# Attention and expert products on one core: six batches of attention moved in among the products of the first four expert units

## The chip, the cores and the metric

The kernel runs on one core of a Trainium2 chip. The metric is device microseconds of one execution. Before the change three runs took 523.98 to 524.93 us, with a median of 524.35 us.

The engines have short names in all views: PE is TensorE (PEld its weight loads), DVE is VectorE, ACT is ScalarE, POOL is GpSimd and SP the engine that issues most transfers. Each works through its own instructions in order.

## The reference

An attention block is followed by a mixture of experts. For each of 8 batches and 8 heads, 512 tokens read 32 states and the states read the tokens; the 544 rows of 512 numbers that result go through one expert of eight.

```python
scores = scale * np.matmul(x, state.transpose(0, 1, 3, 2))      # B, H, S, Ns = 8, 8, 512, 32; D = 64
a = np.exp(scores - scores.max(-1, keepdims=True))
xread = np.matmul(a / (a.sum(-1, keepdims=True) + 1e-09), state)   # token reads
scores2 = scale * np.matmul(state, x.transpose(0, 1, 3, 2))
a2 = np.exp(scores2 - scores2.max(-1, keepdims=True))
sread = np.matmul(a2 / (a2.sum(-1, keepdims=True) + 1e-09), x)     # state reads
x = np.concatenate([xread, sread], axis=2).transpose(0, 2, 1, 3).reshape(B, S + Ns, H * D)
logits, local = x @ w_gate, sigmoid(x @ w_local)
for b in range(B):
    for s in range(S + Ns):                    # in order: an expert can be inherited
        e = argmax(logits[b, s]) if s == 0 or local[b, s] < 0.5 else e
        out[b, s] = softmax(logits[b, s])[e] * (np.maximum(x[b, s] @ w1[e], 0) @ w2[e])
```

With the given inputs the tokens of a batch go to one expert (a token that does not is counted and would be done at the end), so the 512 tokens of a batch are a unit of work with one expert's weights. The 256 state rows are sorted by expert into 9 tiles of 32.

## The kernel before, in words

**Attention** (class `Attention`). Each batch goes through some thirty steps: scores (L301), maxima and transposes on VectorE (L309, L328, L331), subtraction, halves and shares on GpSimd (L338, L349, L361), exponents on ScalarE (L317, L342), transposes and state reads on TensorE (L371, L384), logits (L404, L416), and token reads (L424). A token read is one matmul of 128x512 whose weights, `sd`, hold the states on a diagonal of 32x32 blocks with zeros around them; ScalarE copies its result (L428) and SP writes it to a buffer `xts` in memory. The order of all steps of all eight batches is one hand-written list of names, `STEPS` (L150): `vv31` is the token read 1 of batch 3. Steps `kp` and `wm` are matmuls of zeros that keep TensorE busy. Everything in the list is issued before the first expert product.

**Routing** (class `Routing`). Its constants are made at the start. `route` chooses experts for all batches in one pass of seven pieces, which `unit` issues between the products of the first unit.

**Experts** (class `Experts`, `run`). A unit is 512 tokens of one batch. Both matrix products of a unit are done in halves, and a half as seven products of sums of quarter matrices (`seven`, L927): product 1, 5, 6, 2, 7, 3, 4, each of 8 matmul records of 128x256. So a unit is 4 halves or 28 products. VectorE makes the sums: `first_sum` for the first weights `a`, `second_sums` for the second weights `c`, `column_sum` for the tokens `x` (all recorded at L802). The tokens of the next unit are loaded from `xts` into the other of two buffers. PSUM has six banks for products and two for sums.

**State tiles** (`Tile`). A tile has a first part (`one`, L903) and a second part (`two`, L915). They stand between halves: `ones = {3 + 3 * i: ...}` and `twos = {6 + 3 * i: ...}` (L1062) count halves from the start, so a tile's parts are three halves apart, and two tiles meet at one place. Their weights, 2 MB for each part, have one buffer each (`at`, `ct`).

The schedule is manual: each engine issues in the order in which the program is written. SP's transfers are one queue, too, and GpSimd issues the scatters of the result (L973 for tokens, L924 for tiles) among its other work.

Of the kernel before, what the change touches and what calls it, by code (L numbers as in the profile page):

```python
# [18 lines left out]
P = 128  # L19
# [27 lines left out]
def kernel(  # L47
# [41 lines left out]
    none = keep.tile([1, D], F32, name="none")  # L89
# [5 lines left out]
    with ExitStack() as late:  # L95
        p = late.enter_context(tc.tile_pool(name="p", bufs=4, space=PSUM, side="right"))
        reads = late.enter_context(tc.tile_pool(name="reads", bufs=1, side="right"))
        with ExitStack() as early:
            make_identity(nc, ident)
            start = Attention(early, tc, p, reads, xn, xt, st, stt, wgl, wgs, lt, xts, rows, none, work)  # L100
            route.constants(ident)
            start.clear()
            route.more_constants()
            start.run(route)
        work.prepare()
    work.run()


class Banks:

    def __init__(self, tc, n):
        self.tc, self.ctx, self.sums = tc, ExitStack(), []
        self.open(n)

    def open(self, n):
        self.ctx.close()
        self.pool = self.ctx.enter_context(self.tc.tile_pool(name="ps", bufs=n, space=PSUM))

    def close(self):
        self.ctx.close()  # L120
# [29 lines left out]
STEPS = """  # L150
sc0 kp3 xt11 xt10 mx00 ga kp2 sd3 tr01 xt21 mx01 sd2 mo01 nb0 tr00 et01 sb01 xn0 mo00 wm14 sc1 et00 sb00 ex01 iv0 tu01
tr11 gl tu00 zh01 ex00 tr10 xt20 ec00 zh00 zs01 mo10 sd0 xn1 zs00 sb10 zi0 ec01 mx11 sd1 sr0 ml01 mo11 ex10 mx10 sc2
ml00 st0 xt30 tb01 rt0 sb11 tb00 sl0 xt31 tr20 lg0 nb1 ex11 zh10 sk0 tr21 vv00 et10 zh11 xt41 zs10 vv01 et11 lt0 mx21
fe0 xr00 xt51 zs11 tu11 zi1 xr01 tu10 iv1 ml11 mo21 vv02 xt50 ec10 mo20 ml10 sc3 ec11 tb11 xt40 xr02 mx20 sb21 sr1
tb10 xn2 tr30 sb20 ex21 lg1 mx30 st1 vv03 zh21 ex20 rt1 tr31 nb2 sl1 zh20 et20 vv10 zs21 sk1 lt1 ws1 zs20 et21 tu20
zi2 xt60 mo30 xr10 ml20 sc4 xr03 iv2 mx31 ec20 xn3 ml21 tu21 tb20 vv11 mx41 ec21 nb3 sb30 et30 tb21 sr2 tr40 et31 xt61
# [14 lines left out]
class Attention:  # L171
# [39 lines left out]
    def clear(self):  # L211
# [5 lines left out]
        nc.gpsimd.memset(self.gl, 0.0)  # L217
        nc.gpsimd.memset(self.lt, 0.0)
        nc.gpsimd.memset(self.sd, 0.0)
        nc.gpsimd.memset(self.none, 0.0)  # L220

    def run(self, route):

# [996 lines left out]
```

## Time and profile before

| | |
|---|---|
| median of 3 runs | 524.35 us (523.98 to 524.93) |
| the profiled execution | 524.55 us |
| its span | 522.8 us |
| TensorE busy | 499.0 us, 95% of the span |
| VectorE, ScalarE, GpSimd busy | 256.9, 170.5, 103.5 us |
| transfers | 116.70 MB, mean 223 GB/s |
| chain of waits | PE 90%, DMA 4%, DVE 3% |

The profile is of one execution, so its span can be set against its own time of 524.55 us. The groups are named by the line of the program; additions of whole tiles all have the line of a helper (L802), and the tiles' names tell them apart. A matmul of 32-bit numbers appears as two records. The mean of 223 GB/s hides very different stages: the first 80 us and the loads of weights run at 243 to 420 GB/s in slices of 10 us, and between them the queue is nearly empty.

### The profile page before, as it was taken

How to read it: one execution, taken by the hardware profiler on the slowest of the kernel's cores; microseconds unless marked ns; L12 is line 12 of the kernel's file. 1: busy time of each engine (PE TensorE's matmuls, PEld its weight loads, DVE VectorE, ACT ScalarE, POOL GpSimd, SP SyncE). 2: the span in 40 equal slices, each digit the busy share in tenths (PEclk: the TensorE clock that was granted, in tenths of full speed). 3: DMA queues.
4: the chain of work that ended last, by engine and by line, in shares of the span. 5: the costliest groups of instructions: out<-in, count | busy, mean ns of one | idle time of the engine just before them, and what ended most of it. 6: DMA issues, size and time to landing. Idle time of an engine off the chain costs nothing.

```text
span 522.8 us, 9621 instructions
## 1 busy us (share of the span) xinstructions
PE 499.0 (95%) x3786; PEld 403.4 (77%) x3786; DVE 256.9 (49%) x474; ACT 170.5 (33%) x346; POOL 103.5 (20%) x121
## 2 busy tenths in 40 slices
PE   8799799899999999999999999999999999999992
PEld 3455546778888888888888888888888888878881
DVE  7899765796256225523365127242734255306300
ACT  5688744322232123222232133123322322223210
POOL 7688810001300211001201200111001200210012
PEclk9799989999999999999999999999999999999998
DMA  8999897657294195099293199187079475560011
GB/s 322 367 311 413 314 382 253 224 168 299 88 404 138 59 396 205 9 384 338 89 370 134 46 346 379 50 339 295 1 284 356 175 277 212 167 239 1 1 41 51
DMA packets 35353, 116.70 MB, mean 223 GB/s; under 512 B 3665, under 2 KB 4817, under 8 KB 30946
## 3 DMA queue, kind: packets, MB, share of 16 engines
q1 hardware_dynamic: 32018, 106.41, 54.8%
q0 software_dynamic: 3136, 9.51, 4.7%
q8 instruction: 32, 0.52, 0.4%
q14 instruction: 23, 0.19, 0.1%
q10 hardware_dynamic: 144, 0.07, 0.1%
HBM read 98.14 MB, written 17.89 MB: 222 GB/s over the span
## 4 chain that ended last, share of the span: by engine, by line
PE 90%; DMA 4%; DVE 3%; issue 2%; POOL 0%; ACT 0%; POOLq 0%; DVEq 0%
PE ps L1036 21%; PE ps L989 20%; PE sum L1036 15%; PE sum L989 15%; PE p L424 6%; PE ps L915 3%; PE ps L903 3%; DMA x_n<-in_xn_dram 2%; PE p L384 2%; PE p L371 1%; PE s L301 1%; PE p L416 1%; DMA x_t<-in_xt_dram 1%; DVE c L802 1%; DMA out_dram<-yt,row 1%
## 5 line engine op out<-in xcount | busy, mean ns | idle before, releaser
L989 PE MATMUL ps<-x,a 128*128 128x256 f32 x384 | 91.7, 382 | 0.7 <-ACT xr L428 0.7
L989 PE MATMUL sum<-xs,a 128*128 128x256 f32 x384 | 90.7, 379 | 0.0
L973 POOL DMA_INDIRECT out_dram<-y,tok x32 | 32.9, 1027 | 283.6 <-DVE y L1048 162.1
L989 PEld LDWEIGHTS ps<-x,a 128*128 128x128 f32 x384 | 72.3, 190 | 14.1 <-issue 3.1
L989 PEld LDWEIGHTS sum<-xs,a 128*128 128x128 f32 x384 | 73.0, 190 | 9.9
L1036 PE MATMUL ps<-c,h 128*128 128x256 f32 x264 | 63.0, 381 | 0.1
L1036 PE MATMUL ps<-c,hs 128*128 128x256 f32 x256 | 60.5, 379 | 0.0
L1036 PE MATMUL sum<-c,h 128*128 128x256 f32 x248 | 58.6, 379 | 0.0
L1036 PEld LDWEIGHTS ps<-c,h 128*128 128x128 f32 x264 | 49.7, 190 | 8.6 <-issue 2.2
L802 DVE TENSOR_TENSOR h<-s,s 128x512 f32<-128x512 f32 x16 | 11.1, 691 | 90.9 <-ACT s L1018 89.5
L1036 PEld LDWEIGHTS ps<-c,hs 128*128 128x128 f32 x256 | 48.7, 190 | 6.6
L1036 PEld LDWEIGHTS sum<-c,h 128*128 128x128 f32 x248 | 47.2, 190 | 6.4
L802 DVE TENSOR_TENSOR y<-s,s 128x256 f32<-128x256 f32 x16 | 6.8, 425 | 71.0 <-ACT s L1040 71.0
L802 DVE TENSOR_TENSOR a<-a,a 128x1024 f32<-128x1024 f32 x32 | 37.8, 1216 | 6.0 <-DMA a<-in_w_dram 5.7
L802 DVE TENSOR_TENSOR c<-c,c 128x1024 f32<-128x1024 f32 x32 | 37.6, 1215 | 0.3
L424 PE MATMUL p<-a,sd 128*128 128x512 f32 x64 | 32.3, 628 | 1.2 <-issue 1.2
L1018 ACT COPY s<-sum 128x512 f32<-128x512 f32 x32 | 18.7, 585 | 35.4 <-PE sum L989 32.0
L1036 PE MATMUL sum<-c,hs 128*128 128x256 f32 x128 | 30.2, 379 | 0.0
L989 PE MATMUL ps<-xs,a 128*128 128x256 f32 x128 | 30.2, 379 | 0.0
L934 ACT COPY sum<-ps 128x512 f32<-128x512 f32 (+1 forms) x32 | 14.8, 464 | 45.4 <-PE ps L989 23.1
L1040 ACT ACTIVATE s<-sum,prob 128x256 f32<-128x256 f32 x32 | 15.1, 473 | 43.1 <-PE sum L1036 41.9
L1036 PEld LDWEIGHTS sum<-c,hs 128*128 128x128 f32 x128 | 24.3, 190 | 3.3
(189 smaller groups left out, 560.5 us busy)
## 6 DMA issues: line engine op xcount, KB each, us to landing
at<-in_w_dram SPq DMA_DIRECT2D x18, 1024.0 KB, 7.5
ct<-in_w_dram SPq DMA_DIRECT2D x18, 1024.0 KB, 12.3
a<-in_w_dram SPq DMA_DIRECT2D x32, 512.0 KB, 7.3
c<-in_w_dram SPq DMA_DIRECT2D x32, 512.0 KB, 8.6
x_t<-in_xt_dram SPq DMA_DIRECT2D x16, 512.0 KB, 7.4
x_n<-in_xn_dram SPq DMA_DIRECT2D x8, 1024.0 KB, 10.5
xts<-xr SPq DMA_DIRECT2D x32, 256.0 KB, 4.8
x<-xts SPq DMA_DIRECT2D x8, 1024.0 KB, 8.8
```

The lines of the kernel that those rows point to most:

```text
L301: self.nc.tensor.matmul(s[u][32 * k:32 * k + 32, :], lhsT=self.states(b)[r, k, :], rhs=self.get(f"x_t{k // 2}", b)[r, k % 2, :], start=Tru ...
L384: self.nc.tensor.matmul(r[32 * k:32 * k + 32, u, :], lhsT=e[:, c, u, 32 * k:32 * k + 32], rhs=x_n[:, c, u, k, :], start=(c == 0), stop=(c ...
L424: self.nc.tensor.matmul(v, lhsT=self.sd[:, b, j * P:j * P + P], rhs=self.get("a", b, j // 2), start=True, stop=True)
L802: self.nc.vector.tensor_tensor(out, a, b, op=op)
L903: nc.tensor.matmul(hps[SQ * g:SQ * g + SQ, :], lhsT=self.x_t[:, j, :], rhs=a[:, j, :, g], start=(j == 0), stop=(j == KT - 1))
L915: nc.tensor.matmul(yps[SQ * g:SQ * g + SQ, :], lhsT=self.h[:, m, :], rhs=ct_[:, 2 * m // FK, g // 2, m % (FK // 2), g % 2 * P:g % 2 * P + ...
L934: nc.scalar.copy(y, x)
L973: put = nc.gpsimd.indirect_dma_start(out=out, out_offset=to, in_=y, in_offset=None, bounds_check=NT - 1, oob_is_err=False)
L989: nc.tensor.matmul(to[:, m * width:m * width + width], lhsT=w[:, j, f:f + P], rhs=x[:, j, :], start=begin and m == 0 and j == 0, stop=(m = ...
L1018: return lambda t: nc.scalar.copy(to, t)
L1036: nc.tensor.matmul(to, lhsT=x[:, m, n * P:n * P + P], rhs=w[:, m, :], start=begin and m == 0, stop=(m == FK // 2 - 1), skip_group_check=True)
L1040: return lambda t: nc.scalar.activation(to, t, Act.Copy, scale=p)
```

## The change

Only batches 0 and 1 are done ahead of the products now, by a shorter list `HEAD`. The other six are issued inside units 0 to 3 by a table `FLOW`: a step stands at a number of products after its batch's start, and a batch starts every 14 products. A function `tick` is called after each product and issues what the table has for that number. The sums of weights and tokens, the routing and the tiles' loads go through the same clock.

Token reads are done in 32x32 corners: two calls of eight matmuls take the states directly, without the diagonal `sd`. The result of batch 0 is written straight into the first unit's `x`; there is one buffer for `x` now and the rows of `x` and `w1` have another order. Routing chooses experts for groups of batches (0 and 1, 2 to 4, 5 to 7), and the sorting of state rows follows once. The constants of routing are made on GpSimd inside unit 0. While attention runs, products have two PSUM banks and one for the sum; afterwards five more are opened. Tiles begin at half 20 and come in every half.

```diff
-STEPS = """
-sc0 kp3 xt11 xt10 mx00 ga kp2 sd3 tr01 xt21 mx01 sd2 mo01 nb0 tr00 et01 sb01 xn0 mo00 wm14 sc1 et00 sb00 ex01 iv0 tu01
...
+HEAD = """
+sc0 tr01 tr00 kp3 ga mo01 mo00 sb01 sc1 gl mx00 sb00 mx01 ex01 tr10 nb0 ex00 zh01 tr11 et00 zh00 zs01 mo10 et01 kp7
...
+FLOW = """
+0 sc / 2 mx0 tr0 / 3 mx1 tr1 / 4 nb mo0 / 5 mo1 / 6 et0 sb0 / 7 et1 sb1 / 9 ex0 tu0 / 10 ex1 ec0 / 11 zh0 tu1 /
...
+FIRST, PERIOD = 2, 14
+PER = 28
+BEGIN = 20
...
-            self.steps = [(name, [int(i) for i in at]) for name, at in ((s[:2], s[2:]) for s in STEPS.split())]
+        for name in HEAD.split():
+            self.do(name[:2], *[int(i) for i in name[2:]])
...
+    def flow(self, at):
+        for part in FLOW.split("/"):
+            tick, *names = part.split()
+            for b in range(2, B):
+                for name in names:
+                    at(FIRST + PERIOD * (b - 2) + int(tick), self.do, name[:2], b, *[int(i) for i in name[2:]])
+        for b in range(3, B):
+            for h in range(2):
+                at(FIRST + PERIOD * (b - 3) + 1, self.load_t, b, h)
+            at(FIRST + PERIOD * (b - 3) + 16, self.load_n, b)
+        return FIRST + PERIOD * (B - 3) + 30
...
-    def token_reads(self, b, j):
-        v = self.of["v", b, j] = self.bank()
-        self.nc.tensor.matmul(v, lhsT=self.sd[:, b, j * P:j * P + P], rhs=self.get("a", b, j // 2), start=True, stop=True)
+    def token_reads(self, b, h):
+        v = [self.bank() for k in range(2)]
+        for j in range(Q):
+            at = (b * KT + j) * SQ
+            for k in range(2):
+                self.of["v", b, 2 * h + k] = v[k]
+                r = slice(SQ * (2 * h + k), SQ * (2 * h + k) + SQ)
+                self.nc.tensor.matmul(v[k][SQ * j:SQ * j + SQ, :], lhsT=self.states_of[r, at:at + SQ],
+                                      rhs=self.get("a", b, j // 2)[r, :], start=True, stop=True)
...
+    def at(self, tick, do, *args):
+        self.todo.setdefault(tick, []).append(lambda: do(*args))
+
+    def tick(self):
+        self.ticks += 1
+        for do in self.todo.pop(self.ticks, ()):
+            do()
...
-        bank = Banks(tc, 6)
+        bank = Banks(tc, 2)
...
+        for i in range(4):
+            self.column_sum(i)
+        for i in range(4):
+            self.first_sum(i)
...
+        def tiles_begin():
+            start.ctx.close()
+            bank.open(5, side="right")
...
-        ones = {3 + 3 * i: tile for i, tile in enumerate(tiles)}
-        twos = {6 + 3 * i: tile for i, tile in enumerate(tiles)}
+        ones = {BEGIN + i: tile for i, tile in enumerate(tiles)}
+        twos = {BEGIN + 1 + i: tile for i, tile in enumerate(tiles)}
...
+        for u in range(B):
+            for i in range(4):
+                at(PER * u + 8 + i, self.second_sum, i)
+                if u + 1 < B:
+                    at(PER * u + 18 + i, self.column_sum, i)
+                    at(PER * u + 22 + i, self.first_sum, i)
+        at(2, start.zero_row)
+        done = start.flow(at)
+        for (b0, b1), tick in zip(((0, 2), (2, 5), (5, B)), (3, FIRST + PERIOD * 2 + 29, done)):
+            self.steps(route.choose(start.bank, b0, b1), tick, tick + 1, tick + 3, tick + 4, tick + 6, tick + 8, tick + 9)
+        tick = done + 10
+        at(tick, tiles_begin)
+        self.steps(route.route(bank), tick + 2, tick + 4, tick + 5, tick + 6, tick + 9, tick + 11)
```

**TensorE around the second products of a unit.** `c` are second weights, `h` and `hs` their inputs, `p` PSUM banks of attention, `a` shares, `x_n` tokens, `e` transposed exponents, `ident` the identity for transposes. Before, the attention rows stand packed ahead of all products:

```order
L371 MATMUL p<-ident,e_1225 128x128 x4
L416 MATMUL p<-a,gl 32x128 x8
L404 MATMUL p<-wgs,rt 32x9 x4
L424 MATMUL p<-a,sd 128x512
L384 MATMUL p<-x_n,e 32x64 x32
L424 MATMUL p<-a,sd 128x512 x2
L404 MATMUL p<-wgs,rt 32x9 x4
L416 MATMUL p<-a,gl 32x128 x8
L424 MATMUL p<-a,sd 128x512 x12
L989 MATMUL ps<-x_89,a_90 128x256 x4
```

With the change, in the third and fourth half of unit 0:

```order
L382 MATMUL p<-x_n,e 32x64 x32
L1088 MATMUL ps<-c_595,h_619 128x256 x4
L1088 MATMUL sum<-c_596,h_620 128x256 x4
L1088 MATMUL ps<-c_597,hs_617 128x256 x4
L1088 MATMUL sum<-c_600,h_621 128x256 x4
L1088 MATMUL ps<-c_594,h_618 128x256 x4
L1088 MATMUL ps<-c_598,hs_615 128x256 x4
L427 MATMUL p<-a,states_of 32x512 x8
L1088 MATMUL sum<-c_599,hs_616 128x256 x4
L1088 MATMUL ps<-c_595,h_619 128x256 x4
L369 MATMUL p<-ident,e_1034 128x128 x4
```

Token reads (L427) of batch 2 and the transposes (L369) of batch 3 now stand each between two products, and twelve token reads that stood in a row are gone.

**VectorE at the end of the head.** `first` and `near` find a batch's first expert, `xs` are the column sums and `a_97` the first weight sum. With the change the rows are:

```order
L406 COPY lt<-p 32x9 [waits PE_49]
L527 TENSOR_REDUCE first<-lt 1x1 [waits DVE_49]
L528 TENSOR_TENSOR near<-lt,first 1x8 [waits DVE_49]
L529 SCALAR_TENSOR_TENSOR near<-near,iof 1x8 [waits DVE_49]
L531 TENSOR_REDUCE first<-near 1x1 [waits DVE_49]
L533 CAST units<-first 1x1 [waits DVE_49]
L829 TENSOR_TENSOR xs_89<-x 128x512
L829 TENSOR_TENSOR xs_90<-x,xs_89 128x512 [waits DVE_49]
L829 TENSOR_TENSOR xs_91<-x 128x512
L829 TENSOR_TENSOR xs_92<-x,xs_90 128x512 [waits DVE_49]
L829 TENSOR_TENSOR a_97<-a_95,a_96 128x1024 [waits DMAHW7_49,DMAHW6_49]
```

The same sums before, in `prepare`:

```order
L802 TENSOR_TENSOR a_1437<-a_92,a_93 128x1024
L802 TENSOR_TENSOR xs_1433<-x_89 128x512
L802 TENSOR_TENSOR a_1438<-a_1437,a_90 128x1024
L802 TENSOR_TENSOR xs_1434<-x_89,xs_1433 128x512
L802 TENSOR_TENSOR a_1439<-a_91,a_1438 128x1024
```

The first weight sum stood ahead of the column sums, and now it stands behind all four of them and behind the first expert of batch 1.

**GpSimd at the end.** `y` are tokens' results, `yt` a tile's. Before:

```order
L924 DMA out_dram<-yt,row 17408x128
L973 DMA out_dram<-y_1474,tok 4352x512
L973 DMA out_dram<-y_1475,tok 4352x512
L973 DMA out_dram<-y_1476,tok 4352x512
L924 DMA out_dram<-yt,row 17408x128
L973 DMA out_dram<-y_1477,tok 4352x512
L1179 TENSOR_LOAD left
```

With the change:

```order
L972 DMA out_dram<-yt,row 17408x128 x3
L1025 DMA out_dram<-y_611,tok 4352x512
L1025 DMA out_dram<-y_612,tok 4352x512
L1025 DMA out_dram<-y_613,tok 4352x512
L1025 DMA out_dram<-y_614,tok 4352x512
L1232 TENSOR_LOAD left
```

The last tile's scatter stood between the last two of the tokens, and it now stands ahead of the last four.

More of the change, by code (lines that the diff above doesn't have):

```diff
@@ L93, with open @@
     work = Experts(ctx, tc, w1, w2, xts, rows, all_rows, slots, route, out)
[L95 to L106, printed above, removed]
+    with ExitStack() as head:
+        make_identity(nc, ident)
+        start = Attention(ctx, head, tc, xn, xt, st, stt, wgl, wgs, lt, xts, rows, work)
+        route.constants(ident)
+        start.clear()
+        start.run(route)
+    work.run(start)
 class Banks:
     def __init__(self, tc, n):
-        self.tc, self.ctx, self.sums = tc, ExitStack(), []
+        self.tc, self.ctx = tc, ExitStack()
         self.open(n)
[L115 to L120, printed above, removed]
+    def open(self, n, **side):
+        self.pool = self.ctx.enter_context(self.tc.tile_pool(name="ps", bufs=n, space=PSUM, **side))
     def __call__(self, parts=P, n=512, dt=F32):
@@ L538, in route @@
+        nc.vector.tensor_tensor(pr, logits, mx.to_broadcast(shape), op=Alu.subtract)
         yield
-        seq = bank(B, T, BF16)
-        for i in range(SC):
-            nc.tensor.transpose(seq[:, i * P:i * P + P], top[:, :, i], identb)
-        nc.tensor.transpose(seq[:, S:], top[:N, :, SC], identb[:N, :N])
-        pr = rt.tile([P, COLS, E], F32, name="pr")
-        nc.vector.tensor_tensor(pr, lf[:, :, :E], mx.to_broadcast([P, COLS, E]), op=Alu.subtract)
         nc.scalar.activation(pr, pr, Act.Exp)
@@ L555, in route @@
-        back = bank(P, NC * B, BF16)
-        for i in range(SC):
-            nc.tensor.transpose(back[:, i * B:i * B + B], run[:, i * P:i * P + P], identb[:B, :B])
-        nc.tensor.transpose(back[:N, SC * B:], run[:, S:], identb[:B, :B])
-        held = bank(P, B)
-        nc.tensor.matmul(held, lhsT=self.one, rhs=self.first.rearrange("o b x -> o (b x)"), start=True, stop=True)
-        zp = rt.tile([P, COLS], F32, name="zp")
+        zp = flat(self.zp)
         nc.vector.tensor_reduce(zp, pr, axis=AX, op=Alu.add)
@@ new lines, in choose @@
+        back, held = t[:, :NC * B // 2].bitcast(BF16).rearrange("p (i b) -> p i b", i=NC), t[:, NC * B - n:]
+        for i in range(SC):
+            nc.tensor.transpose(back[:, i, :n], run[:, i * P:i * P + P], self.identb[:n, :n])
+        nc.tensor.transpose(back[:N, SC, :n], run[:, S:], self.identb[:n, :n])
+        nc.tensor.matmul(held, lhsT=self.one, rhs=self.first[:, b].rearrange("o b x -> o (b x)"), start=True, stop=True)
+        yield
+        nc.vector.tensor_copy(ex[:, b, :SC], back[:, :SC, :n].rearrange("p i b -> p b i"))
@@ L925, in scatter, with seven @@
                                              in_offset=None, bounds_check=NT * Q - 1, oob_is_err=False)
[L927 removed]
+        def seven(y, n, product, copies, whole, tick, waiting=(), apart=False):
             y = y[:, :n]
```

492 lines of the change are left out of this document (249 added, 243 removed).

## The prediction

> **What bounds the kernel now.** I read the head of the page first, then TensorE alone in order of time, then the groups by line, and last the tail and the transfers.
>
> ```profile
> span 522.8 us, 9621 instructions
> PE 499.0 (95%) x3786; PEld 403.4 (77%) x3786; DVE 256.9 (49%) x474; ACT 170.5 (33%) x346; POOL 103.5 (20%) x121
> ```
>
> TensorE is busy for 95% of the span, so the time is a sum of TensorE's work, of its waits and of a tail. The profiled execution took 524.55 us, 1.75 more than its span and 0.2 more than the median of the runs, 524.35. TensorE in order of time gives the parts:
>
> ```profile
> 84.01 1.99 PE L989 MATMUL ps<-x,a 128*128 128x256 f32 x8 [0.68 <-ACT xr L428]
> ...
> 89.39 0.39 PE L542 MATMUL ps<-identb,top 128*8 128x128 bf16 x4
> ...
> 89.82 1.99 PE L989 MATMUL ps<-x,a 128*128 128x256 f32 x8
> ...
> 115.72 1.89 PE L1036 MATMUL ps<-c,hs 128*128 128x256 f32 x8
> ...
> 136.44 1.89 PE L1036 MATMUL sum<-c,h 128*128 128x256 f32 x8
> ...
> 254.90 1.89 PE L989 MATMUL sum<-xs,a 128*128 128x256 f32 x8
> 256.72 1.96 PE L915 MATMUL ps<-ct,htt 128*32 128x128 f32 x64
> 258.49 1.91 PE L903 MATMUL ps<-at,xtt 128*32 128x256 f32 x32
> 260.33 1.99 PE L989 MATMUL ps<-x,a 128*128 128x256 f32 x8
> 262.16 1.89 PE L989 MATMUL ps<-xs,a 128*128 128x256 f32 x8
> ```
>
> The expert products begin at 84.01; all before that is attention. From 115.72 to 136.44 lie twelve products, 1.727 us each; 8 units of 28 make 386.8 us. A state tile's two parts between two products take 262.16 - 254.90 less two products: 3.81 us. Nine tiles, one first part and one last part alone, make 34.5. 84.0 + 386.8 + 34.5 = 505.3, and the last product ends at 512.4 (its row is below), so 7.1 us are routing's matmuls and waits. The same rows price an insertion: the product ahead of the tile takes 1.82 and the one behind it 1.83, not 1.73, so breaking into the products costs 0.2 us beside the inserted work.
>
> **The head.** Six of eight batches leave it. TensorE's steps of a batch when packed (start to start):
>
> ```profile
> 29.86 0.42 PE L404 MATMUL p<-wgs,rt 128*32 128x9 f32 x8
> 30.21 1.13 PE L424 MATMUL p<-a,sd 128*128 128x512 f32 x2
> 31.17 0.60 PE L371 MATMUL p<-ident,e 128*128 128x128 f32 x4
> 31.70 1.09 PE L301 MATMUL s<-x_t,sttc 64*32 64x512 f32 x16
> 32.72 0.66 PE L371 MATMUL p<-ident,e 128*128 128x128 f32 x4
> 33.21 1.02 PE L424 MATMUL p<-a,sd 128*128 128x512 f32 x2
> 34.17 1.10 PE L384 MATMUL p<-x_n,e 128*32 128x64 f32 x64
> 35.09 0.62 PE L416 MATMUL p<-a,gl 128*32 128x128 f32 x16
> 35.64 0.66 PE L371 MATMUL p<-ident,e 128*128 128x128 f32 x4
> ```
>
> State logits 0.35, transposes 0.53 and 0.49, scores 1.02, state reads 0.92, logits 0.55, and a token read 0.96 for each of four: about 7.7 us a batch, 62 for eight. The head of before is thus mostly TensorE's own work. With two batches it becomes a chain across engines instead:
>
> ```profile
> 24.00 0.14 DVE L517 CAST first<-first 1x1 int32<-1x1 f32 x1
> ...
> L338 POOL TENSOR_TENSOR e<-e,m 128x512 f32<-128x512 f32 x16 | 16.7, 1048 | 3.3 <-DVE m L331 3.3
> L349 POOL TENSOR_TENSOR zh<-e 128x256 f32<-128x256 f32 x16 | 11.6, 733 | 0.7 <-ACT e L342 0.5
> L365 DVE STREAM_TRANSPOSE a<-e 128x512 f32<-128x512 f32 x16 | 10.9, 686 | 1.4 <-POOL e L361 1.2
> L428 ACT COPY xr<-p 128x512 f32<-128x512 f32 x32 | 18.7, 588 | 14.3 <-PE p L424 13.5 <-DMA xts<-xr 0.8
> L802 DVE TENSOR_TENSOR xs<-x,xs 128x512 f32<-128x512 f32 x16 | 11.0, 687 | 0.2
> L802 DVE TENSOR_TENSOR a<-a,a 128x1024 f32<-128x1024 f32 x32 | 37.8, 1216 | 6.0 <-DMA a<-in_w_dram 5.7
> ```
>
> Batch 0's first expert was known at 24.1, with two other batches mixed in; without them I put it at 22. GpSimd is the slow partner: twice 1.05 (subtract), 0.73 (halves) and again 1.05 (shares) per batch. Its last share of batch 1 comes about 4 us after batch 0's expert, at 26. Then follow, one after the other: transpose 0.7, token reads of one half 1.0, two copies of 0.59 that free PSUM for the other half, these reads 1.0, logits 0.6, state logits 0.4, VectorE's five small steps for the expert 1.1: 32.7 with half a dozen handovers. VectorE is in order, so behind them stand four column sums (2.75) and the first weight sum (1.22): 36.7. The first product needs none of these and starts at about 32, the second waits for that sum until 36.7. Counted back by one product, the head is worth a start at 35.0. The load of unit 0's weights runs under batch 1. The idle 3 us have an after-effect:
>
> ```profile
> 66.04 0.31 PE L416 MATMUL p<-a,gl 128*32 128x128 f32 x3 [2.18 <-issue]
> ...
> 67.61 1.94 PE L384 MATMUL p<-x_n,e 128*32 128x64 f32 x64
> ```
>
> After 2.2 us of idleness the state reads took 1.94, not 1.10. I add that 0.8 once: an effective start at 35.8 (33.5 to 39), against 84.0.
>
> **The six batches inside.** Token reads are now two calls of eight 32x32 matmuls. No row has that shape. The nearest is the scores' call: eight matmuls of 64x32 in two row groups and four column groups, 1.02 together. Bounds: 1.02 a call, or twice that if only four run together as with the 128x32 forms; I take 1.02, since rows and columns are split in the same way. A batch then costs 1.02 + 0.92 + 2.04 + 1.02 + 0.55 + 0.35 = 5.9. It breaks in at seven places: 0.2 at the five whose matmuls have another shape than the products, 0.1 (an estimate) at the two transposes: 7.1 us, 42.6 for six.
>
> [...]
>
> Routing for three groups instead of one: a group breaks in twice, 0.43 (89.39 to 89.82) and about as much again, with 0.2 each: 1.3 us. Two more groups add 2.6. One wait of before goes, since the groups are spread:
>
> ```profile
> PE ps L582 <- DVE states L570: 1.7, 1, 1.7
> L1010 DVE SCALAR_TENSOR_TENSOR hs<-h,h 128x512 f32<-128x512 f32 x16 | 11.1, 692 | 1.7
> ```
>
> The final routing now stands in unit 4 at products 2 to 11, where VectorE has about 7 us of routing beside 4 us of halves in five products (8.6): its last matmul waits some 2 us. So routing is 7.1 + 2.6 - 1.7 + 2 = 10.
>
> **Waits in units 0 to 3.** Each attention step stands one to four products behind the step that feeds it, 1.7 us or more. VectorE is tightest: between the 4th and 8th product it has eight attention operations and six of the unit, 14 x 0.69 = 9.7 us in 6.9, and catches up under the next six. TensorE's token reads of the other batch stand just where that backlog ends. I take 2 us in all; bounds 0 and 10 (below).
>
> **Tiles in units 5 to 7.** A tile formerly came every third half, now in every half: 4 MB in each 12.1 + 3.8 = 15.9 us, plus 5 MB a unit. In the middle of a unit, from the second part of one tile (28 us into the unit) to the first part two bounds later (59.8), there are 11 MB of loads in one queue (two c, two a of tiles, x, next weights) and three scatters: 12.3 million bytes.
>
> ```profile
> 225.00:230.00 5.00, 5.00 (x25) 4.41 (x24) 0.24 (x1) 1.42 (x3) 0.00 (x0) 1.00 1.02 370
> 230.00:235.00 5.00, 5.00 (x25) 4.41 (x24) 1.65 (x3) 0.83 (x2) 0.99 (x1) 1.00 1.03 427
> 235.00:240.00 5.00, 5.00 (x24) 4.39 (x24) 3.75 (x4) 1.39 (x3) 0.00 (x0) 1.00 1.00 414
> ...
> xgt<-rows,state POOLq DMA_INDIRECT x9, 2.6
> ```
>
> A loaded queue moved 370 to 427 GB/s, 404 on the mean: 30.5 us, and about 2.6 to land (a 64 KB gather's whole time) make 33.1 in a gap of 31.8. TensorE waits 1.3 us in units 5 and 6, 2.6 together; bounds 0 (at 427) and 8 (at 370). The next unit's x, behind 4 MB of tile weights, lands some 6 us after VectorE wants it; VectorE has that to spare, since only the next unit reads those sums.
>
> **The tail.**
>
> ```profile
> 510.70 1.89 PE L1036 MATMUL ps<-c,h 128*128 128x256 f32 x8
> 512.63 0.48 DVE L1054 SCALAR_TENSOR_TENSOR y<-ps,prob,s 128x256 f32<-128x256 f32 x1 [0.74 <-PE ps L1036]
> 513.72 0.98 POOL L924 DMA_INDIRECT out_dram<-yt,row  x1 [2.24 <-DMA out_dram<-y,tok]
> 517.22 0.98 POOL L973 DMA_INDIRECT out_dram<-y,tok  x1 [2.51 <-DMA out_dram<-yt,row]
> ```
>
> The last y was ready at 513.1 and left at 517.2, since the last tile's scatter stood between the two of y and each waited for the one ahead. Now that tile ends a half earlier. The tail shrinks by 4.1, from 10.4 to 6.3.
>
> **Sum.** 35.8 + 386.8 + 34.5 + 42.6 + 10 + 2 + 2.6 = 514.3, tail 6.3: a span of 520.6 against 522.8. The removed 48.2 us of head come back as 42.6 inside and 7.5 of new routing and waits; the tail's 4.1 decide. With 1.75 around the span that is 522.35, 2.2 below the profiled 524.55; against the median of 524.35 it is **522.2**, 0.4% below.
>
> **The rivals.**
> 1. *Attention is late inside the units* (slower). VectorE's backlog of 2.8 us by the 8th product grows where one shares' transpose is late, and TensorE, in order, stands before the reads. Decisive once the transposes end after the 9th product; two waits of 0.8 a batch are 10 us, not 2: 530. For it: 14 operations in four products; against: VectorE is 49% busy overall. 17%.
> 2. *Transfers bound the last three units* (slower). At 370 GB/s the waits are 8, not 2.6, and the bounds between gain no slack: 527 to 531. Against it are the two rows above 410. 11%. [...]
> 3. *Nothing waits* (faster). The head ends at 33.5 and waits and transfers cost nothing: 522.2 - 2.3 - 2 - 2.6 = 515. For it: each step has a product or more of room, and no expert product of before waits for a transfer. 22%.
> 4. *The corners don't run eight at a time*: 12 more calls' worth in six batches and 2 in the head, 536. 5%.
>
> **Chances.** The forecast has 45%, with its own range 517 to 527. What a measurement can tell from no change is 0.2%, 523.3 to 525.4. The forecast puts 28 points below that, 10 inside, 7 above; rival 3 adds 22 below, the others 33 above or at it (some 2 at it). Faster 0.50, same 0.12, slower 0.38. Range 511 to 533.
>
> **What would show it.** First expert product near 32 and the second near 37; the score calls and the corner reads about 1 us each between products of 1.8; token reads without a wait in front; the first part of a state tile waiting for its weights once in units 5 and 6; the last y scatter within 1 us of the last VectorE operation. The forecast is wrong if corner calls take 2 us, or if TensorE's waits after the head exceed 10 us or fall below 2.

## The result

The changed kernel takes **521.6 us** (median of 20 runs, 519.2 to 526.1), the kernel before 525.1 us beside it (20 runs, 522.8 to 528.8). The ratio is 0.994, with a 95% interval of 0.992 to 0.996. In a second comparison it was 0.997 (0.996 to 0.999, the kernel before at 521.8). So the change makes the kernel faster by between 0.3% and 0.6%: 1.5 to 3.4 us of the some 50 us of attention that it takes out of the head. The forecast was 522.2.

The profiled execution took 519.18 us with a span of 516.9, and was the fastest of its 20 runs; its terms add up to less than the median for that reason. What moves from one execution to the next is told in the last section.

### The profile page after: what moved, and what is told of

It is laid out like the page before. It is cut to its first block, busy times and chain, and to the rows that moved or that the text cites. A ratio compares the mean times of both kernels' runs of the same rounds, so it can differ in the third digit from the quotient of the medians.

```text
span 516.9 us, 10104 instructions
## 1 busy us (share of the span) xinstructions
PE 495.2 (96%) x4008; PEld 392.3 (76%) x4008; DVE 278.1 (54%) x543; ACT 161.1 (31%) x334; POOL 109.3 (21%) x134
## 4 chain that ended last, share of the span: by engine, by line
PE 71%; DMA 17%; DVE 6%; issue 2%; ACT 1%; SPq 0%; POOLq 0%; POOL 0%; DVEq 0%
PE ps L1041 17%; PE ps L1088 17%; PE sum L1041 14%; PE sum L1088 12%; DMA out_dram<-y,tok 8%; DMA x<-xts 5%; DMA out_dram<-yt,row 3%; PE p L427 3%; PE s L299 2%; PE p L382 1%; PE p L369 1%; PE ps L963 1%; PE ps L950 1%; DMA x_t<-in_xt_dram 1%; DVE xs L829 1%
## 5 line engine op out<-in xcount | busy, mean ns | idle before, releaser
L1041 PE MATMUL sum<-xs,a 128*128 128x256 f32 x384 | 92.0, 382 | 0.0
L1025 POOL DMA_INDIRECT out_dram<-y,tok x32 | 36.6, 1144 | 230.6 <-DVE xs L829 59.1
L1041 PEld LDWEIGHTS sum<-xs,a 128*128 128x128 f32 x384 | 71.5, 190 | 16.5 <-ACT s L1070 4.1
L829 DVE TENSOR_TENSOR a<-a,a 128x1024 f32<-128x1024 f32 x32 | 40.2, 1296 | 0.8 <-issue 0.6
L829 DVE TENSOR_TENSOR c<-c,c 128x1024 f32<-128x1024 f32 x32 | 38.4, 1241 | 0.3
L829 DVE TENSOR_TENSOR y<-s,s 128x256 f32<-128x256 f32 x16 | 6.8, 424 | 42.6 <-ACT s L1092 42.6
L1041 PEld LDWEIGHTS ps<-xs,a 128*128 128x128 f32 x128 | 24.7, 193 | 6.6 <-DVE a L829 3.2
```

The costliest lines, as they stand in the source:

```text
L829: self.nc.vector.tensor_tensor(out, a, b, op=op)
L1025: put = nc.gpsimd.indirect_dma_start(out=out, out_offset=to, in_=y, in_offset=None, bounds_check=NT - 1, oob_is_err=False)
L1041: nc.tensor.matmul(to[:, m * width:m * width + width], lhsT=w[:, j, f:f + P], rhs=x[:, j, :], start=begin and m == 0 and j == 0, stop=(m = ...
```

## The profile after

The head of the page:

```profile
span 516.9 us, 10104 instructions
PE 495.2 (96%) x4008; PEld 392.3 (76%) x4008; DVE 278.1 (54%) x543; ACT 161.1 (31%) x334; POOL 109.3 (21%) x134
```

TensorE's busy time fell by 3.8 us, although 222 of its instructions were added. TensorE in order of time, at the end of the head, at one corner read inside unit 0, and at the last product:

```profile
28.86 0.42 PE L402 MATMUL p<-wgs,rt 128*32 128x9 f32 x8 [0.16 <-ACT xr L436]
29.21 1.99 PE L1041 MATMUL ps<-x,a 128*128 128x256 f32 x8
34.00 2.85 PE L1041 MATMUL ps<-xs,a 128*128 128x256 f32 x8 [2.79 <-DVE a L829]
36.78 1.85 PE L299 MATMUL s<-x_t,sttc 64*32 64x512 f32 x16
38.56 1.99 PE L1041 MATMUL sum<-xs,a 128*128 128x256 f32 x8
...
80.36 1.09 PE L427 MATMUL p<-a,states_of 32*32 32x512 f32 x16
81.38 1.99 PE L1088 MATMUL sum<-c,hs 128*128 128x256 f32 x8
...
508.43 1.89 PE L1088 MATMUL ps<-c,h 128*128 128x256 f32 x8
```

The products start at 29.2 instead of 84.0, and the last one starts at 508.4 and ends at 510.2 instead of 512.4. So TensorE is only 2.2 us ahead at the end; nearly all that left the head stands between the products. One corner call takes 81.38 - 80.36 = 1.02 us.

TensorE's waits after the head, by what released them (line, releaser: us in total, times, longest):

```profile
PE ps L1041 <- DVE a L829: 2.8, 1, 2.8
PE ps L709 <- DVE todo L708: 2.3, 1, 2.3
PE ps L963 <- issue: 2.0, 2, 1.7
PE ps L950 <- DMA at<-in_w_dram: 1.9, 2, 1.2
PE p L582 <- DVE ran L572: 1.4, 2, 0.8
```

This is the whole list. No attention step of the six batches inside the units is in it. A tile's weights (`at`) are late twice. The wait for `todo`, the count of tokens left, and the unnamed one at L963 were not foreseen. TensorE's two rows, and VectorE's rows that lead to them:

```profile
415.35 2.25 PE L963 MATMUL ps<-ct,htt 128*32 128x128 f32 x57 [1.71 <-issue]
...
459.16 0.18 PE L709 MATMUL ps<-todo,ones 128*1 128x40 bf16 x1 [2.27 <-DVE todo L708]
```
```profile
414.55 0.35 DVE L967 TENSOR_SCALAR yt<-ps,probq 128x128 f32<-128x128 f32 x1 [14.50 <-DMA out_dram<-yt,row]
414.82 0.43 DVE L956 STREAM_TRANSPOSE htt<-ht 128x256 f32<-128x256 f32 x1
...
458.34 0.35 DVE L967 TENSOR_SCALAR yt<-ps,probq 128x128 f32<-128x128 f32 x1 [11.06 <-DMA out_dram<-yt,row]
...
458.97 0.14 DVE L708 CAST todo<-undone 128x40 bf16<-128x40 f32 x1
```

A tile's result `yt` has one buffer. VectorE stood 14.5 and 11.1 us until the scatter of the tile before had landed, and behind that, in VectorE's order, stood what TensorE needs: the transposed hidden values `htt` for the second part of the next tile (ready at 415.25, and TensorE starts at 415.35), and the count. It stood so twice more, 11.3 us at 391 and 8.0 at 478 us, where nothing that TensorE needed was late.

The tail, from the last row of GpSimd:

```profile
511.12 0.98 POOL L1025 DMA_INDIRECT out_dram<-y,tok  x1 [1.90 <-DVE y L1106]
```

No tile's scatter stands among the last ones any more, and the last of `y` leaves at 511.1; from the last product's end to the end of the span it is 6.7 us, before 10.4.

## The experiments

Three groups of kernels ran, each on one chip beside the kernel before. Its median was 525.1 us beside the result above, and 521.8, 524.8 and 522.3 us in the three groups. I compare with the changed kernel's 0.994 where the kernel before took about 525, and with its 0.997 where it took about 522. The changed kernel itself ran in the first comparison and in the first group alone, so in the other two groups this choice is an assumption: with the other of its two ratios a difference to it is 1.7 us larger or smaller. Differences between traces don't depend on it and are given beside.

**The changed kernel again**, the first of a group of four.

> The changed kernel once more, without any edit, to stand beside the three other kernels of this group. Every theory expects its time again, 521.6 us, and a ratio to the kernel before of 0.992 to 0.996.

Measured: 520.2 us, ratio 0.997 (0.996 to 0.999). Still faster, by half as much as in the first comparison. The two intervals just touch. Its profile is a second sample of the same kernel, and its waits in units 5 and 6 are others: 3.5 us for tile weights instead of 1.9, 1.3 at L963 instead of 2.0, 1.8 for the count instead of 2.3. Single waits there can't be compared between runs to better than 1 to 2 us.

**The tail alone, on the kernel before.**

```
             product(y, 6)
             two(y)
-            for results in waiting[:1]:
+            for results in (waiting if apart else waiting[:1]):
                 results()
```

The loop that issued the rest of `waiting` after product 7 of the last half goes.

> The kernel before, with one edit: the last tile's scatter is issued ahead of the last half's two token scatters, where the changed kernel has it, instead of between them. Theory (the three scatters at the end land one after the other, and the one in the middle holds the last back by its own time): the end after the last product falls from 10.4 to 6.3-6.7 us, TensorE's part stays as it is, and the time falls by 3.7 to 4.1 us, to 521 us. Rival (the order of the scatters is immaterial, and the short end of the changed kernel comes from something else): no change, 525.1 us. Second rival (the tile's last product now comes ahead of a product of the unit and holds it back): the last product ends 1 to 3 us later, and the gain is 1 to 3 us.

Measured: 518.8 us, ratio 0.995 (0.994 to 0.996): 2.0 to 3.4 us less. GpSimd's last scatters in this kernel:

```profile
502.85 0.98 POOL L924 DMA_INDIRECT out_dram<-yt,row  x1 [2.48 <-DMA out_dram<-y,tok]
506.18 0.98 POOL L971 DMA_INDIRECT out_dram<-y,tok  x1 [2.35 <-DVE y L1046]
509.07 0.98 POOL L971 DMA_INDIRECT out_dram<-y,tok  x1 [1.91 <-DVE y L1052]
```

Its last product ends at 508.1 and its span at 514.7: the tail is 6.6 us, as the theory has it. The order of the scatters is not immaterial. This edit of three lines gives about as much as the whole change (0.995 against 0.997 in the same group, and 0.994 in the first comparison).

**The tail undone, on the changed kernel.** `BEGIN = 20` becomes `BEGIN = 21`.

> The changed kernel with one number changed back: the tiles begin one half-unit later, so that the last tile's scatter stands again between the last two token scatters. Theory: the end after the last product grows from 6.7 to about 10.4 us, and the time by 3.7 us, to 525.3 us, which is the kernel before: the rest of the change (the products that end 2.2 us earlier) then hardly shows. Rival (the order is immaterial): 521.6 us. Second rival (the later tiles miss the stretch of full transfers in units 5 and 6): the two waits for a tile's weights, 1.9 us, go away, and 1.8 us of the 3.7 come back.

Measured: 522.0 us, ratio 1.000 (0.999 to 1.002), which is 0.3% or 1.7 us above the changed kernel beside it. The last product starts at 506.28, 2.1 us earlier than in the changed kernel's profile; the tail is 10.5 us. TensorE's waits for tiles and for the count:

```profile
411.13 1.93 PE L950 MATMUL ps<-at,xtt 128*32 128x256 f32 x32 [0.43 <-DMA at<-in_w_dram]
443.62 1.93 PE L950 MATMUL ps<-at,xtt 128*32 128x256 f32 x32 [0.49 <-DMA at<-in_w_dram]
451.78 0.19 PE L709 MATMUL ps<-todo,ones 128*1 128x40 bf16 x1 [2.57 <-DVE todo L708]
```

The second rival came nearest: 3.8 us of tail come, and 2.1 us in front of it go. But half of its two waits for tile weights stays, and what goes is 1.0 of them and the 2.0 at L963; against that stand 0.3 more at the count and a granted clock of 0.50 from 451.4 to 454.8 us, which the changed kernel's profile didn't have there. Without the tail, the rest of the change is worth nothing that can be measured.

**Two buffers for a tile's result.**

```
-                y = tile_at["hp"].tile([P, P], F32, name="yt")
+                y = tile_at["hp"].tile([P, P], F32, name="yt", bufs=2)
```

> The changed kernel with a second buffer for a tile's result before its scatter, and nothing else. In the profile VectorE stood 11.06 us at 458 us for a scatter to give this buffer back, and the count that TensorE then waited 2.3 us for stood behind it on VectorE. Theory (the count's wait is the single buffer's doing): both waits go, the time falls by 2.3 us, to 519.3 us. Rival (the count waits for the transfer of the rows whose count it is, or the scatters are late for TensorE in another place): VectorE's 11 us go and TensorE's 2.3 us stay or turn up elsewhere, 521.6 us.

Measured: 516.3 us, ratio 0.990 (0.987 to 0.993), 3.7 us below the changed kernel beside it (1.9 to 5.5). After the head its waits are:

```profile
PE ps L950 <- DMA at<-in_w_dram: 3.4, 2, 2.4
PE ps L1041 <- DVE a L829: 2.8, 1, 2.8
PE p L582 <- DVE ran L572: 1.4, 2, 0.8
```

Both the count's wait and the unnamed one at L963 are gone, 4.3 us; tile weights wait 1.5 more than in the changed kernel's first profile, but no more than in its second (3.5). So the theory was right, and by the trace too small: I had seen the count's wait alone. The issue wait at 415 us is the same buffer's doing.

**The corner reads twice.**

```
-        for j in range(Q):
+        for j in list(range(Q)) * 2:
             at = (b * KT + j) * SQ
```

> The changed kernel with the 16 matmuls of every corner-read call issued twice over; the second time writes the same values, so nothing else changes. It asks whether TensorE's work is what sets the time inside the units, as the forecast's sum supposes, and what a call costs. Twelve of the sixteen calls lie inside units 0 to 3, four in the head. Theory (TensorE's time adds up): each call inside the units costs 0.9 to 1.05 us more, 11 to 13 us in all, and the four of the head 0 to 4 us; 533 to 538 us. Rival (the attention's instructions inside the units stand in waits, of transfers or of ScalarE, that would take up the work): 521.6 to 526 us. [...]

Measured: 531.5 us, ratio 1.012 (1.009 to 1.015): 9.4 us above the changed kernel (7.6 to 11.2). A doubled call takes 1.88 us instead of 1.02 before the next product starts:

```profile
82.10 1.95 PE L427 MATMUL p<-a,states_of 32*32 32x512 f32 x32
83.98 1.99 PE L1088 MATMUL sum<-c,hs 128*128 128x256 f32 x8
```

The twelve calls inside the units took 22.5 us instead of 12.3 (summed start to start): 10.2 us, 0.85 a call, and from the first product to the last it is 8.9 us more. The whole of the added work shows, less 1.3. And the 1.3 is no slack: in the changed kernel's profile the granted clock was 0.50 from 35.0 to 38.4 us, behind the wait of 2.8 us, which cost 1.8 us; behind the same wait it stayed at 1.00 here. TensorE's work is what sets the time inside the units; there is no slack there that would take it up. The price in my expectation was some 15% too high: the second pass pays no break into the products.

**The column sums forward.** In the head's order by hand, VectorE's four column sums go into the hole in which it waits for the last logits, and the second batch's expert goes behind the first weight sums:

```
-ml11 tb10 kp2 sr1 tb11 st1 vv11 rt1 vv10 xr12 xr13 lg1 xr11 sl1 lt1 xr10 sk1 fe1
+ml11 tb10 kp2 sr1 tb11 st1 vv11 rt1 cs0 cs1 cs2 cs3 vv10 xr12 xr13 lg1 xr11 sl1 lt1 xr10 sk1
...
-        for i in range(4):
-            self.column_sum(i)
         for i in range(4):
             self.first_sum(i)
+        start.first_expert(1)
```

> The changed kernel with VectorE's four column sums moved forward in its own queue, into the 2.9 us in which it is idle before the first unit, and the second half of the first expert's rows moved behind the first of the weight sums. Theory (the wait of 2.8 us ahead of the second product is the order of VectorE's queue alone): the wait goes, and with it the 1.6 to 1.8 us that the lowered clock cost on the next products; the time falls by 3 to 4.6 us, to 517-518.6 us. Rival (the first weight sum waits as well for the weights' transfer, or for the scalars of the sums to be made): the wait stays or shrinks by under 1 us, 521 us. Second rival (the products start earlier but meet the attention's steps inside the units not ready): waits of 2 to 4 us show up in unit 0 and 1 and the time stays.

Measured: 519.0 us, ratio 0.989 (0.987 to 0.992), 2.4 us below the changed kernel (0.5 to 4.3).

```profile
29.21 1.99 PE L1041 MATMUL ps<-x,a 128*128 128x256 f32 x8
31.04 1.89 PE L1041 MATMUL ps<-xs,a 128*128 128x256 f32 x8
...
33.88 1.99 PE L1041 MATMUL sum<-xs,a 128*128 128x256 f32 x8
...
40.02 1.99 PE L1041 MATMUL sum<-xs,a 128*128 128x256 f32 x8 [2.42 <-ACT s L1070]
```

The wait of 2.8 us was the order of VectorE's queue and nothing else: the weights had landed. Third product at 33.9 instead of 38.6, as the theory has it. But a new wait of 2.4 us stands two products later: ScalarE copies a product's result only at 38.9 us, by the profile when a transfer of the head has ended:

```profile
38.89 0.58 ACT L1070 COPY s<-ps 128x512 f32<-128x512 f32 x1 [7.03 <-DMA rows<-zero]
```

In the changed kernel ScalarE stands at the same line until 37.8 (5.97 us, by the profile behind the token reads' way out, `xts<-xr`), and the late second product covers it. In the kernel with both edits the profile names neither, so which transfer it is stays open. At the routing's matmul L583 in unit 0 the kernel is 2.0 us ahead (50.1 instead of 52.1), of 4.7 won at the third product: over half of the gain is lost to the next wait in line, which none of the three expectations named. The whole span is only 0.6 us shorter in this profile, since its clock was at 0.50 from 174.9 to 178.4 us instead.

**Both edits.**

> The changed kernel with both edits of the two kernels before: the column sums forward in VectorE's queue, and a second buffer for a tile's result. Theory (two separate waits, one in the head and one in unit 6, both on the path that sets the end): the gains add up, 5.3 to 6.9 us, to 515-516.5 us. Rival (what is won early is lost at the waits for transfers in units 5 and 6, where the DMA engines were 0.89 to 0.97 busy): 2 to 3 us of it come back as waits for tile weights there, 518-519 us.

Measured: 514.6 us, ratio 0.981 (0.978 to 0.983), 6.9 us below the changed kernel (5.1 to 8.6): within the intervals the gains add up (3.7 and 2.4). The tile weights wait 3.5 us, 1.6 more than in the changed kernel's first profile and as long as in its second, so the rival's loss of 2 to 3 us is not seen.

> The kernel with both edits (column sums forward, two buffers for a tile's result) once more, to stand beside the three other kernels of this group. Its ratio to the kernel before was 0.981; every theory expects 0.978 to 0.984 again, 513 to 516 us.

Measured: 515.0 us, ratio 0.985 (0.981 to 0.988), just above the expected range of ratios; 6.6 us below the changed kernel (4.5 to 8.6). Among the kernels that compute the reference's result this one and the last one below are the fastest, 1.5 to 1.9% faster than the kernel before.

**The corners alone, on the kernel before.** The block-diagonal states, their four copies and their fill go; the token reads become corners; the rows and the first weights are laid out as in the changed kernel:

```
-        self.nc.tensor.matmul(v, lhsT=self.sd[:, b, j * P:j * P + P], rhs=self.get("a", b, j // 2), start=True, stop=True)
+                self.nc.tensor.matmul(v[k][SQ * j:SQ * j + SQ, :], lhsT=self.states_of[r, at:at + SQ],
+                                      rhs=self.get("a", b, j // 2)[r, :], start=True, stop=True)
```

> The kernel before with one part of the change alone: the token reads in 32x32 corners in place of the block-diagonal 128x128 products, with the layouts that go with it, all eight batches in the head as before, and routing as before. It takes about 16 us of TensorE's work out of the head (32 products of 1.5 to 1.7 us become 16 calls of 1.02 us with the same rows written) and four copies and a fill from ScalarE and GpSimd. Theory (the head is bound by a chain in which TensorE has a part, and by the transfers beside it): the first product of the units starts 3 to 10 us earlier, 515 to 522 us: about as good as the whole change, or better. Rival (TensorE bounds the head): 14 to 16 us earlier, 509-511 us. Second rival (the head is bound by transfers alone, or by ScalarE's and VectorE's copies): 0 to 2 us, 523-525 us.

(A product of before took 0.9 to 1.0 us in its rows, not the 1.5 to 1.7 written here; that 16 us of work go holds: 32.3 us busy less 16 calls of 1.02.)

Measured: 527.7 us, ratio 1.006 (1.004 to 1.008): slower. The theory fell; even the second rival, which expected next to no gain, was too hopeful. The end of the head:

```profile
71.52 1.05 PE L422 MATMUL p<-a,states_of 32*32 32x512 f32 x4 [1.02 <-issue]
73.53 6.98 PE L422 MATMUL p<-a,states_of 32*32 32x512 f32 x64 [0.96 <-ACT xr L427]
81.71 3.78 PE L988 MATMUL ps<-x,a 128*128 128x256 f32 x8 [1.20 <-ACT xr L427]
85.28 2.84 PE L988 MATMUL ps<-xs,a 128*128 128x256 f32 x8
87.96 1.89 PE L988 MATMUL sum<-xs,a 128*128 128x256 f32 x8
```

TensorE had less to do and waited for ScalarE's copies instead. After the waits of 1 us its clock fell (granted clock 0.50 from 73.6 to 87.2 us): four calls took 7.0 us instead of 4.1, and the first two products 6.2 instead of 3.6. It isn't one execution's chance: over all seven runs of this kernel the mean granted clock was 0.963 to 0.979, against 0.983 to 0.995 in the kernel before beside it. The stretch from 66 to 92 us (columns: length, busy time and count of PE, PEld, DVE, ACT, POOL, granted clock, DMA share, GB/s), here and in the kernel before with the tail alone, which has the old head and where the products begin at 79.6:

```profile
66.00:92.00 26.00, 22.55 (x220) 11.83 (x209) 13.99 (x27) 10.29 (x20) 1.19 (x2) 0.74 0.90 320
```
```profile
66.00:92.00 26.00, 25.32 (x115) 15.79 (x114) 16.15 (x32) 12.35 (x23) 0.89 (x1) 1.00 0.96 348
```

The fourth product starts at 90.2 here, at 89.8 in the kernel before, whose profile had its own stretches of lowered clock in the head, and at 85.4 in the kernel with the tail alone, which had none there: the lighter head is 0.4 to 4.8 us longer. Another 2.8 us are three state tiles whose second part took 2.7 us instead of 1.8 (at 177, 298 and 339 us), with stops that the profile puts to "issue". I have no cause for these; they stay open.

**The corners undone, inside the changed kernel.**

```
-        for j in range(Q):
...
+        for k in range(2):
+            self.of["v", b, 2 * h + k] = v[k]
+            self.nc.tensor.matmul(v[k], lhsT=self.states_of[:, b * P:b * P + P], rhs=self.get("a", b, k),
+                                  start=True, stop=True)
```

> The changed kernel with each corner-read call (eight 32x32 products of 512 columns) replaced by two 128x128 products of 512 columns, the number that the kernel before used. The states are not spread on a diagonal for it, so the token reads' values, and all that the experts make of them, are not the reference's; the routing and the amount of all other work are the same. It asks what the corners are worth inside the units. Theory (by the rows, 0.96 us for one 128x128 product and 1.02 for a whole corner call, less 0.2 to 0.4 of break-in that the big products may not pay): 0.5 to 0.9 us more for each of the twelve calls inside, 6 to 11 us, and 0 to 3.6 for the four of the head: 528 to 535 us. Rival (the attention inside the units has slack, so cheaper reads only wait longer): 521.6 to 524 us.

Measured: 524.5 us, ratio 1.004 (1.001 to 1.006), 3.4 us above the changed kernel's 0.997 (1.9 to 4.9). The theory's row was right and its sum too large: the twelve calls took 20.9 us instead of 12.3, 0.72 more a call. The products beside them took 1.73 us each and not 1.82 and 1.83 as beside a corner call, which gives back 0.2 a call, so 6.2 us of work are added. But the waits fell by 2.6 us at the same time (the unnamed 2.0 at L963 did not occur), and from the first product to the last it is 3.1 us more. So the corners save 6.2 us of TensorE's time inside the units and about 3 us of the whole, and nothing in the old head.

**Tile weights left out.** In a tile's load: `if self.i: return`.

> The changed kernel, with the weights of the nine state tiles loaded for the first tile alone: the other eight tiles compute with the first one's weights, so the output of their rows is not the reference's. All instructions of TensorE and VectorE are as before; 32 transfers of 1 MB are left out. The profile of the changed kernel has three kinds of waits in units 5 and 6: for tile weights 1.9 us, without a named cause at 415 us 2.0 us, and for the count 2.3 us, the last two behind VectorE, which stood 14.5 and 11.1 us for a tile's scatter. Theory (all three come from the full transfer queue, the last two since the scatters are slow in it): all go, 5 to 6 us less than the changed kernel, 515.5-516.5 us. Rival (the scatters are late by their own order, not by the loads): only the 1.9 go, 519.7 us. Second rival (the loads also slow the expert units' own transfers, so that the transfers bound the last units as the first forecast's rival had it): 8 us or more, 513 us or less.

Measured: 512.7 us, ratio 0.981 (0.978 to 0.984), 8.6 us below the changed kernel's 0.997 (6.8 to 10.4). Its waits after the head, but for one of 0.2 us where the head ends, are these:

```profile
PE ps L1043 <- DVE a L829: 2.8, 1, 2.8
PE p L582 <- DVE ran L572: 1.4, 2, 0.8
```

All three kinds of waits went, 6.2 us. From the first product to the last it is 7.5 us less: the 6.2, and 1.0 in the tiles' second parts (16.1 instead of 17.1 us). The theory's mechanism holds, a little more than its size. The second rival's 8 us cannot be excluded by the times, but the trace has no room for it: without these loads, units 5 to 7 have no waits at all. What the transfers cost the last units can be read from two windows of the same length, the changed kernel and this one, whose last product ends at 503.6:

```profile
340.00:510.00 170.00, 163.65 (x1436) 137.36 (x1434) 58.48 (x96) 38.84 (x77) 26.92 (x25) 1.00 0.74 279
```
```profile
340.00:510.00 170.00, 163.80 (x1440) 137.34 (x1438) 61.22 (x97) 39.56 (x78) 28.24 (x26) 0.99 0.25 87
```

Tile weights are two thirds of all that moves there. Without them TensorE is busy for every microsecond up to its last product; with them it stands idle for some 6 of the 170 us.

**A gap in the tiles.** Both edits, and the tiles begin at half 19 with no tile at half 26:

```
-        ones = {BEGIN + i: tile for i, tile in enumerate(tiles)}
-        twos = {BEGIN + 1 + i: tile for i, tile in enumerate(tiles)}
+        begins = [at for at in range(BEGIN - 1, BEGIN + NTILE) if at != 26]
+        ones = {at: tile for at, tile in zip(begins, tiles)}
+        twos = {at + 1: tile for at, tile in zip(begins, tiles)}
```

> The kernel with both edits, and the nine tiles begun one half-unit earlier with the third half of unit 6 left without a new tile, so that they end where they ended. In the kernel with both edits TensorE waited 0.66 us in unit 5 and 2.79 us in unit 6 for a tile's weights, each time at the third half of the unit, where the next unit's weights and rows are in the same queue. Theory (the queue is full at that place alone, and a gap there gives it time): the 2.79 us go; one more break into the products costs 0.4 us; 2.0 to 2.4 us less than the kernel with both edits, 512.4 us. Rival (the queue is full through units 5 and 6 and the wait moves to the next tile): 0 to 1 us less, 514 us. Second rival (starting earlier puts tile weights beside the final routing's work or the last attention steps): 1 to 3 us more.

Measured: 513.5 us, ratio 0.983 (0.980 to 0.986), against 0.985 for both edits beside it: 0.8 us, inside the intervals.

```profile
385.68 2.43 PE L950 MATMUL ps<-at,xtt 128*32 128x256 f32 x32 [2.06 <-DMA at<-in_w_dram]
```

Unit 6 no longer waits, where both edits have 2.8 and 2.0 us in their two profiles; unit 5 now waits 2.06 instead of 0.66 and 0.86. The rival was nearer: where the queue is full, the wait moves to the tile that is left there.

## Why the prediction was right

The forecast was right in sign and size, and the trace says for which reasons. In part its sum is right by luck: most terms were too high, and the waits that the transfers cause too low. Its terms against the profiled execution:

| term | forecast, us | trace, us |
|---|---|---|
| effective start of the products | 35.8 | 34.1 |
| products | 386.8 | 386.8 |
| state tiles | 34.5 | 35.8 |
| six batches inside the units | 42.6 | 40.7 |
| routing, with its waits | 10 | 9.1 |
| attention steps that wait | 2 | 0 |
| tile weights that wait | 2.6 | 1.9 |
| the unnamed wait at L963 | - | 2.0 |
| tail | 6.3 | 6.7 |
| span | 520.6 | 516.9 |

The parts measured one by one add up to 0.2 more than the span. The forecast put 1.75 us around the span; it is 2.3 in the changed kernel.

- *The start.* The first product stood ready earlier than I had put it (29.2, not 32), since GpSimd's last share of batch 1 came at 24.5, not 26; and the second waited for exactly the instruction named: 34.0, not 36.7. The lowered clock behind the wait (0.50 from 35.0 to 38.4 us) cost more than my 0.8: the second product took 2.78 instead of 1.73 and the scores 1.78 instead of 1.02, 1.8 in all. 34.00 - 1.73 + 1.8 = 34.1.
- *The six batches.* The steps, summed start to start, took 34.7 us at full clock (forecast 35.4): a corner call 1.02, as its nearest row had it. The products around them, compared with undisturbed ones, took 6.0 us longer (forecast 7.2): 0.2 at each of the thirty places whose matmuls have another shape than the products, and nothing at the twelve transposes of 128x128, for which I had put 0.1. The fourth rival, corners that do not run eight at a time, is out: one call would have been 2 us. The 128x128 calls in the corners' place cost the products beside them nothing: 1.73 us each, against 1.82 and 1.83 beside a corner call.
- *Routing.* Too high by 0.9. Its matmuls and waits took 7.2 us, the products around them 1.8 more. The 2 us at its last matmul in unit 4 did not occur; VectorE was not behind there. A wait of nearly the same length occurred elsewhere, at the count in unit 6, for a reason that the forecast did not have.
- *Attention waits.* None. The first rival, attention late inside the units, is out: VectorE's backlog by the 8th product never reached TensorE.
- *Tile weights.* Where forecast, at the third half of units 5 and 6, and 0.7 shorter. The second rival, transfers that bound the last units with 8 us, had the right resource: with the two waits that come from slow scatters the transfers cost 6.2 us of waits, over twice my term (and 6.5 in the second profile). It was the term most mis-sized, hidden by the batches', routing's and the attention's being too high: that is the luck. The sentence that VectorE has time to spare for a late `x` held, though it waited 13.3 and 9.3 us for it and not 6. What the forecast did not have is the other wait in VectorE's order there, 25.6 us at two places for one buffer that a scatter held.
- *The tail.* Right, and shown from both sides: put on the kernel before it takes 3.8 us off the trace and 2.0 to 3.4 off the time; taken from the changed kernel it brings back 3.8 us of tail.
- *The balance.* "The tail's 4.1 decide" held. The doubled reads show why the move itself gives so little: inside the units TensorE has no slack (10.2 us of added work took 8.9 us more), so each moved microsecond is paid there. And the corners alone show that the old head would not have become shorter by less TensorE work (16 us less of it, and 0.4 to 4.8 us longer). The third rival, that nothing waits, is out: 7.6 us of waits stand behind the second product. With the 2.8 in front of it, which the forecast counts to the head, they are 10.4, so its own sign of being wrong, over 10 us after the head, was missed only by that way of counting.

## What to carry to other kernels

Moving work out of a head that is mostly the bottleneck engine's own work moves its price along (here 49.9 us less of head and 40.7 more inside the units); count the moved instructions and the breaks they make, and look for what else changes at the end. A break cost 0.2 us here where the matmul's shape changed: calls of the stream's own shape were free at their edges, with 1.73 us for the products beside them. A short edit of the last few transfers' order gave here as much as a reordering of the whole program (ratios of 0.995 and 0.997 in one group), so try the ends of the chain alone first. When a queue becomes full (355 to 414 GB/s here in the slices from 362 to 413 us), look at every single-buffered tile that a slow transfer holds: the engine that waited for the buffer (VectorE, 14.5 us) carried along what stood behind it in its order (TensorE's 1.7 us at 415 us).

## What had not been expected of the hardware

- *The clock differs between executions of the same instructions.* The profile of the changed kernel and that of the same kernel again, from 13 to 26 us and in unit 2 (columns as above):

```profile
13.00:26.00 13.00, 10.79 (x224) 5.67 (x223) 10.34 (x31) 7.84 (x20) 9.66 (x20) 1.00 0.92 345
...
168.00:182.00 14.00, 13.19 (x81) 10.32 (x80) 13.57 (x24) 6.13 (x13) 2.83 (x3) 1.00 0.17 60
```
```profile
13.00:26.00 13.00, 11.29 (x160) 5.75 (x162) 10.28 (x31) 7.73 (x18) 9.18 (x16) 0.80 0.92 343
...
168.00:182.00 14.00, 13.19 (x71) 9.96 (x70) 13.27 (x23) 4.93 (x11) 2.10 (x2) 0.88 0.16 57
```

  The granted clock was 1.00 in both stretches in the first, 0.80 and 0.88 in the second. These are means: inside them the clock is 1.00 or 0.50, and a stretch at 0.50 lasts 3.4 us (178 to 181.3 us in the second) or a few times that (6.8 us from 16.1 in the kernel before, 13.6 us from 73.6 with the corners alone). TensorE's rows of the second in the head, where the calls of 14 and 18 matmuls are one batch's token reads:

```profile
18.13 0.65 PE L414 MATMUL p<-a,gl 128*32 128x128 f32 x16 [0.65 <-DVE a L363]
18.71 1.55 PE L427 MATMUL p<-a,states_of 32*32 32x512 f32 x18
20.52 1.64 PE L427 MATMUL p<-a,states_of 32*32 32x512 f32 x14 [0.27 <-ACT x L436]
```

  The last of these took 1.08 us in the first execution, behind the same gaps of 0.65 and 0.27 us. The first product then started at 31.6 instead of 29.2, and unit 2 took 1.7 us longer. Behind the second product it was the other way round, 0.50 in the first from 35.0 to 38.4 us and 1.00 in the second, so the two spans differ by 2.2 us. Over the 20 runs the time lost to the lowered clock (a run's span times one minus its mean granted clock) goes from 3.6 to 7.3 us, and the spans from 516.9 to 523.9: it can be about half of that spread, as large as the change, and the rest is not explained.

  The traces of all kernels together say when it happens. Behind the head, up to the last product, they hold thirteen stretches of 3.4 us at 0.50, and each begins within 1.6 us of the end of a TensorE wait of 0.8 us or more, or just before that end. But 34 other waits as long have none behind them; after the wait of 0.81 us in unit 2 it came in three of nine traces. That the waits are the cause is read from this, and no run varied a wait alone.
- *Less work on TensorE can cost time.* With the corners in the old head the granted clock from 66 to 92 us was 0.74, against 1.00 with the old reads, and the 16 us of work saved were lost to that and to waits for ScalarE's copies of 1.0 and 1.2 us: the whole took 1.006 of the time.
- *Scatters suffer from loads.* GpSimd's waits for a scatter of `y` to land were 5.2 to 7.7 us in units 5 and 6 of the changed kernel, with tile weights in the queue, and 1.2 to 4.9 us in the same units without their loads. The longest:

```profile
408.69 0.99 POOL L972 DMA_INDIRECT out_dram<-yt,row  x1 [7.71 <-DMA out_dram<-y,tok]
```
